# Attention and Hyena gate on one core: q loaded in 1 KB runs with strided PSUM writes, all row maxima in one TensorE transpose, and a new instruction order

## The chip, the cores and the metric

The kernel runs on one core of a Trainium2 chip. The metric is device time in microseconds; smaller is better. PE is TensorE, PEld its weight loads, DVE is VectorE, ACT is ScalarE, POOL is GpSimd and SP is SyncE, which here only issues DMAs. A time quoted below is a median of several runs; a profile is one execution, some 2 us shorter than the time of the same run, because it counts from the first to the last instruction. The profiled execution of the kernel before took 383.55 us, less than any of its timed runs, so its page shows that kernel at its best.

## The reference, cut to what matters

Eight batches of eight heads, 576 rows, head width 64, float32 in and out. First linear attention with a feature map that subtracts the row's largest absolute projection, then a Hyena layer on the result:

```python
def phi(x):
    proj = np.einsum('bhsd,df->bhsf', x, w_phi)
    proj = proj - np.max(np.abs(proj), axis=-1, keepdims=True)
    return np.concatenate([np.exp(proj), np.exp(-proj)], axis=-1)
q_p, k_p = phi(q), phi(k)
kv = np.einsum('bhsf,bhsd->bhfd', k_p, v)
z = np.sum(k_p, axis=2)
num = np.einsum('bhsf,bhfd->bhsd', q_p, kv)
den = np.einsum('bhsf,bhf->bhs', q_p, z)[..., None] + 1e-06
# x = num / den, heads joined to 512 columns; then for each batch
x1, x2, x3 = split(x @ w_proj, 3)
x2_conv = irfft(rfft(x2) * rfft(filter))       # along the 576 rows
out = (x1 * x2_conv * x3) @ w_out
```

The order of rows is free for k and v, because they are summed over rows. It isn't free for q: the result's rows enter a Fourier transform.

## The kernel before: the parts that matter

A "unit" is half a batch (four heads), so there are 16. The program fixes for each engine the sequence of its instructions. The kernel builds a list of about 2,500 named nodes and emits them by a literal table `ORDER`; a second table, `SLOTS`, says which of the eight PSUM banks each result uses. Both came from an offline planner.

k and v are loaded with four consecutive rows per partition, 1 KB runs in DRAM. q keeps plain row order (chunk `ci` holds rows 128 ci to 128 ci + 127), and so has 256-byte runs and four loads:

```python
def main(dst, src, g0, g1):                      # k and v
    nc.gpsimd.dma_start(
        out=dst[:, g0:g1].rearrange("p g h c d -> p (g h) (c d)"),
        in_=src[b, 4 * g0:4 * g1, 0:512, :].rearrange("h (p c) d -> p h (c d)", c=4))
def f_q(ci, g0, g1):                             # q, for ci in range(4)
    def f():
        nc.gpsimd.dma_start(
            out=c.qs[:, g0:g1, :, ci].rearrange("p g h d -> p (g h) d"),
            in_=q[b, 4 * g0:4 * g1, ci * P:(ci + 1) * P, :].rearrange("h p d -> p h d"))
```

The maximum of each row of q is found with rows on the partitions, but has to be subtracted with features on the partitions. It is split into two bf16 parts (`M2`), transposed by a DMA (by PE in the first two units), and subtracted by a matmul that accumulates onto the projection in PSUM. (It is subtracted twice over because the first exponential reads the bank before the subtraction: both exponentials of a row then carry the same factor, which cancels in `num / den` but for the 1e-06.)

```python
nc.sync.dma_start_transpose(out=c.mT[i2], in_=c.M2[i2].rearrange("p c h e -> p (c h e)"))
def f_pqa(hp, j):                                # the projection
    def f():
        pp = c.bank(f"{n}pq{hp}{j}", [P, 4, P], FP32)
        for e in range(2):
            nc.tensor.matmul(pp[:, e:4:2, :], lhsT=c.wpp[:, e * P:(e + 1) * P],
                             rhs=qT(hp + 2 * j), start=(e == 0), stop=True, ...)
def f_pqb(hp, j):                                # minus twice the maximum
    def f():
        nc.tensor.matmul(c.open[f"{n}pq{hp}{j}"].rearrange("f c p -> f (c p)"),
                         lhsT=c.sel[:, 2 * hp + j, :],
                         rhs=c.mT[i2][:, 0:4, :].rearrange("p c q -> p (c q)"),
                         start=False, stop=True, ...)
def f_q(hp, j, sg):                              # ScalarE: exp of the bank
    def f():
        nc.scalar.activation(E("q" + "pm"[sg], hp)[:, j],
                             c.open[f"{n}pq{hp}{j}"].rearrange("f c p -> f (c p)"),
                             AF.Exp, bias=0.0, scale=(1.0, -1.0)[sg])
```

Two more places matter. POOL weights v by the maxima of k, 96 multiplies that read SBUF (L765 and L805). DVE multiplies spectra with the filter, both operands in SBUF (L1031, and the sums of its products at L1037):

```python
nc.gpsimd.tensor_tensor(out=v12[:, sg, :, 0:HD]..., in0=c.vs[b % 2][...], in1=v12[..., 64:65]..., op=ALU.mult)
TT(out=p[:, sl, :], in0=c.CS[:, sl, :], in1=H[:, sl, :], op=ALU.mult)      # TT = nc.vector.tensor_tensor
```

Of the kernel before, what the change touches and what calls it, by code (L numbers as in the profile page):

```python
# [16 lines left out]
P = 128  # L17
# [31 lines left out]
class Node:  # L49
# [3 lines left out]
    def __init__(self, name, eng, ns, need, fn, take=(), use=(), lat=0, tab=0, at=0.0):  # L53
        self.name, self.eng, self.ns, self.need, self.fn = name, eng, ns, list(need), fn
        self.take, self.use, self.lat, self.tab, self.at = list(take), list(use), lat, tab, at

# [17 lines left out]
def const_nodes(c, w_phi, w_proj, filt, w_out):  # L74
# [21 lines left out]

    def f_sel():

        c.sel = tile_([P, 4, P], "sel")
        nc.vector.memset(c.sel, 0.0)  # L100
        for h in range(4):
            nc.vector.memset(c.sel[32 * h:32 * h + 2, h, :], -2.0)

    def f_m2():
        c.M2, c.mxq = [], []
        for i in range(2):
            t = tile_([P, 5, 4, 32], f"M2_{i}")
            nc.vector.memset(t, 0.0)
            c.M2.append(t)
            t = tile_([P, 5, 4], f"mxq_{i}", FP32)  # L110
            nc.vector.memset(t, 0.0)
            c.mxq.append(t)
# [29 lines left out]
    A("sel", "DVE", 950, [], f_sel)  # L142
    A("M2z", "DVE", 820, [], f_m2)
# [16 lines left out]
    def f_w(g, j):  # L160
        def f():
            if (g, j) == (0, 0):
                c.wproj = tile_([P, 4, 1536], "wproj")
            nc.gpsimd.dma_start(out=c.wproj[64 * j:64 * j + 64, 2 * g:2 * g + 2, :],
                                in_=wv[g, j])
        return f
# [12 lines left out]
    for g in range(2):  # L179
        for j in range(2):  # L180
            A(f"wi{g}{j}", "POOL", 680, ["wi00"] if g + j else [], f_w(g, j))
            A(f"w{g}{j}", "DMA", 2200, [f"wi{g}{j}"], None, lat=6000)
# [4 lines left out]
def trig_nodes(c):  # L187
# [118 lines left out]
    A("thalf", "DVE", 800, [f"t{i}{j}" for i in range(2) for j in range(2)], f_half)  # L306
# [11 lines left out]
def fold_nodes(c, name, need, need_g, get_x, get_eo, get_G, k0, at=None):  # L318
# [19 lines left out]
    def rem():  # L338
# [3 lines left out]
    c.add(n + "f1", "DVE", dve2(578), need, level1(0, ALU.add))  # L342
    c.add(n + "f2", "DVE", dve2(578), need, level1(1, ALU.subtract))
    c.add(n + "f3", "DVE", dve2(580), [n + "f1", n + "f2"] + need_g,
          level2(slice(0, 4, 3), ALU.add))
    c.add(n + "f4", "DVE", dve2(580), [n + "f1", n + "f2"] + need_g,
          level2(slice(1, 3), ALU.subtract))
    c.add(n + "fr", "DVE", 113, [n + "f3", n + "f4"], rem)
# [23 lines left out]
def spectrum_nodes(c):  # L372
# [93 lines left out]
    for i in range(2):  # L466
        A(f"f.swi{i}", "SP", 80, ["f.fix4"], f_sw(i))
        A(f"f.sw{i}", "XB", 100, [f"f.swi{i}"], None, lat=2500)
    A("f.cp0", "DVE", 345, ["f.S2", "f.S3"], f_cp(0))
    A("f.cp1", "DVE", 345, ["f.S0", "f.S1", "f.fix0"], f_cp(1))  # L470
# [15 lines left out]
def load_nodes(c, b, q, k, v):  # L486
# [18 lines left out]
    def f_q(ci, g0, g1):  # L505
        def f():
            nc.gpsimd.dma_start(  # L507
                out=c.qs[:, g0:g1, :, ci].rearrange("p g h d -> p (g h) d"),
                in_=q[b, 4 * g0:4 * g1, ci * P:(ci + 1) * P, :].rearrange("h p d -> p h d"))
        return f  # L510
# [16 lines left out]
    for (g0, g1) in ([(0, 1), (1, 2)] if b == 0 else [(0, 2)]):  # L527
# [12 lines left out]
        dma("k", 830, wk, f_k(g0, g1), 1400 * w)  # L540
        for hp in range(2):
            dma(f"kt{hp}", 600, wk, f_t(lambda: c.kt, k, hp, g0, g1), 200)
        for ci in range(4):
            dma(f"q{ci}", 750 if w == 1 else 865, wq, f_q(ci, g0, g1), 600 * w)
        for hp in range(2):
            dma(f"qt{hp}", 620, wq, f_t(lambda: c.qt, q, hp, g0, g1), 200)
        c.now = t0 + (2.0 if b == 0 else 8.0)
        dma("v", 830, wv, f_v(g0, g1), 1400 * w)
        for g in gs:
            for hp in range(2):  # L550
                dma(f"vt{hp}{g}", 590, wv + ["vtz"], f_vt(hp, g), 100)
        if b:
# [11 lines left out]
            A(n + "kx", "XB", 2500, [n + "kxi"], None, lat=2500)  # L564
            wx = [f"a{2 * b - 4 + i}.{x}{h}{j}" for i in range(2) for h in range(2)
                  for j in range(2) for x in ("pqa", "qn")] if b > 1 else []
            A(n + "qxi", "SP", 1300, [f"{s}q{i}" for i in range(4)] + wx,
              f_x(lambda: c.qT, lambda: c.qs))
            A(n + "qx", "XB", 2500, [n + "qxi"], None, lat=2500)
# [7 lines left out]
            A(n + "txi", "SP", 1600, [f"{s}{x}{h}" for x in ("kt", "qt") for h in range(2)] + wx,  # L577
              f_tx)
            A(n + "tx", "XB", 1000, [n + "txi"], None, lat=2500)
# [3 lines left out]
def attn_nodes(c, t, tune):  # L583
# [31 lines left out]
    if b == 0:  # L615
# [32 lines left out]
        A(n + "qtp", "PE", 8 * mm(P), [f"{l}q{i}" for i in range(4)] + ["ident"],  # L648
# [51 lines left out]
    def f_mx0():  # L700
        nc.vector.tensor_copy(c.M2[i2][:, :, :, 0], mxq())

    def f_mx1():
        nc.vector.tensor_tensor(out=c.M2[i2][:, :, :, 1], in0=mxq(),
                                in1=c.M2[i2][:, :, :, 0], op=ALU.subtract)

    def f_mt():
        nc.sync.dma_start_transpose(out=c.mT[i2],
                                    in_=c.M2[i2].rearrange("p c h e -> p (c h e)"))

    at(4.5)
    A(n + "mx0", "DVE", 80, [f"{n}qm{hp}{j}" for hp in range(2) for j in range(2)] + [n + "tm"]
      + unit("mt"), f_mx0)
    A(n + "mx1", "DVE", 100, [n + "mx0"], f_mx1)
    sels = ["tlb"] + [f"pqb{hp}{j}" for hp in range(2) for j in range(2)]
    if t in c.pe_mt:
        def f_mtp():
            tp = c.bank(n + "mtp", [P, 5, P], BF16)
            for ci in range(5):
                nc.tensor.transpose(tp[:, ci, :],  # L720
                                    c.M2[i2][:, ci].rearrange("p h e -> p (h e)"), c.ident)

        def f_mtc():
            nc.vector.tensor_copy(c.mT[i2], c.open[n + "mtp"])
        A(n + "mtp", "PE", 5 * mm(P), [n + "mx1", "ident"], f_mtp, take=[n + "mtp"])
        A(n + "mt", "DVE", dve2(640), [n + "mtp"] + unit(*sels), f_mtc, use=[n + "mtp"])
    else:
        A(n + "mti", "SP", 1300, [n + "mx1"] + unit(*sels), f_mt)
        A(n + "mt", "XB", 1600, [n + "mti"], None, lat=2400)
# [43 lines left out]
    for hp in range(2):  # L773
# [9 lines left out]
        for sg in range(2):  # L783
            A(f"{n}c{sg}{hp}", "ACT", 95, [f"{n}ra{hp}0", f"{n}ra{hp}1"]
              + back(hp, ["kv{}"]), f_c(hp, sg), tab=TAB_EXP)
            A(f"{n}v{sg}{hp}", "POOL", pool(512), [f"{n}c{sg}{hp}", vl] + back(hp, ["kv{}"]),
              f_v(hp, sg), lat=70)
# [28 lines left out]
    def f_tlb():  # L816
        for j in range(2):
            nc.tensor.matmul(c.open[n + "tq"][:, j, :], lhsT=c.sel[:, j, :],
                             rhs=c.mT[i2][:, 4, :], start=False, stop=True,
                             skip_group_check=True)  # L820
# [9 lines left out]
    for sg in range(2):  # L830
# [5 lines left out]
          + unit("kv0", "kv1"), f_vt(sg), lat=70)  # L836
# [7 lines left out]
    def f_pqa(hp, j):  # L844
        def f():
            pp = c.bank(f"{n}pq{hp}{j}", [P, 4, P], FP32)
# [6 lines left out]
    def f_pqb(hp, j):  # L853
        def f():
            nc.tensor.matmul(c.open[f"{n}pq{hp}{j}"].rearrange("f c p -> f (c p)"),
                             lhsT=c.sel[:, 2 * hp + j, :],
                             rhs=c.mT[i2][:, 0:4, :].rearrange("p c q -> p (c q)"),
                             start=False, stop=True, skip_group_check=True)
        return f

    def f_q(hp, j, sg):
        def f():
            nc.scalar.activation(E("q" + "pm"[sg], hp)[:, j],
                                 c.open[f"{n}pq{hp}{j}"].rearrange("f c p -> f (c p)"),
# [64 lines left out]
    for hp in range(2):  # L929
        at(12.0 + 4 * hp)  # L930
        A(f"{n}kv{hp}", "PE", 20 * mm(65), [f"{n}{x}{hp}{j}" for x in ("e0", "e1")
# [5 lines left out]
        for j in range(2):  # L937
            k = f"{n}ne{hp}{j}"
            A(k, "PE", 10 * mm(65), [f"{n}kvs{hp}", f"{n}q0{hp}{j}", f"{n}q1{hp}{j}",
# [37 lines left out]
    else:  # L977
# [11 lines left out]
        A(n + "xx", "XB", 2200, [n + "xxi"], None, lat=2400)  # L989
    A(n + "x0", "DVE", 80 if t in c.pe_xt else 170, [n + x for x in xx], f_x0)  # L990
# [6 lines left out]
def moe_nodes(c, b, out_b, tune):  # L997
# [62 lines left out]
    for i in range(2):  # L1060
        A(f"{n}p{i}4", "DVE", dve2(512), [n + "cs4"]
          + prev(*[f"{'ab'[i]}{m}" for m in range(4)]), f_p(i, slice(4, 5)))
        A(f"{n}p{i}0", "DVE", dve2(1024), [n + "cs0", n + "cs1"] + prev(f"y{i}"),
          f_p(i, slice(0, 2)))
        A(f"{n}p{i}2", "DVE", dve2(1024), [n + "cs2", n + "cs3"] + prev(f"y{i}"),
          f_p(i, slice(2, 4)))
        A(f"{n}y{i}", "DVE", dve2(1024), [f"{n}p{i}0", f"{n}p{i}2"]
          + prev(*[f"{'ab'[i]}{m}" for m in range(4)]), f_y(i))
# [71 lines left out]
    for m in range(4):  # L1140
        def old2(ev):
# [12 lines left out]
          + prev(*[f"fi{i}" for i in five], d=2), f_yt(m))  # L1154
# [35 lines left out]
PE_MT = (0, 1)  # L1190
SLOTS = (
    "0123456720436140177625763745703754167426342647536201364570127302731456136125473532514351"
    "0642571065063013407543750237564276512630754613750621357317420756210505301635023750375312"
    "0152407120435612074360254102346102541054073215637127251675162514365234614506150732410357"
    "2057142536721540673214671536725041741672376241072610421407531426730453156320514731247653"
    "0124604167231540732626253057126045724607236415072037132570650713560427601452761457350724"
    "3671045045365413061061064056235042573462517043214536751406732510465265401252475472315436"
    "0146210346245246325763415672014750132061423705612306453405340534057321467530217460")
ORDER = [
    74, 11, 6, 75, 7, 90, 94, 1, 88, 78, 86, 26, 0, 40, 27, 383, 64, 52, 66, 54, 30, 55, 53,  # L1200
    42, 32, 67, 50, 65, 16, 38, 28, 34, 4, 36, 33, 51, 2, 29, 43, 41, 31, 39, 35, 37, 5, 3,
    60, 58, 62, 18, 56, 12, 68, 22, 14, 20, 46, 44, 17, 76, 82, 96, 8, 77, 477, 481, 387, 482,
    384, 81, 385, 386, 403, 391, 63, 59, 57, 61, 84, 87, 97, 91, 95, 80, 83, 92, 93, 89, 79,
    13, 15, 388, 392, 478, 404, 389, 407, 395, 393, 390, 394, 396, 415, 497, 479, 419, 501,
    480, 498, 416, 420, 410, 409, 405, 427, 430, 428, 499, 417, 422, 500, 406, 503, 418, 449,
    397, 398, 408, 399, 98, 485, 437, 99, 109, 100, 400, 486, 101, 483, 110, 102, 413, 431,
# [261 lines left out]
```

## Time and profile before

| | before |
|---|---|
| time, median of 4 | 390.04 us (387.0 to 391.36) |
| profiled span (of a run of 383.55 us) | 381.4 us |
| PE, DVE, ACT, POOL busy | 83%, 85%, 71%, 49% |
| granted TensorE clock, mean | 0.955 |

From the page of the kernel before: the busy table, the row of the granted clock in 40 slices (tenths of full speed), and the chain of waits, followed back from the last instruction.

```profile
PE 318.3 (83%) x3071; PEld 198.3 (52%) x3071; DVE 324.2 (85%) x732; ACT 271.6 (71%) x667; POOL 188.5 (49%) x236
...
PEclk9998698898999999999999996998999999999999
...
DVE 41%; PE 37%; DMA 9%; ACT 6%; POOL 3%; issue 3%; DVEq 0%; ACTq 0%; POOLq 0%
```

No engine is full, and the chain changes hands between DVE and PE. The table of stretches, for the whole middle (start and end, length, busy time of each engine with its instruction count, clock, DMA share, GB/s):

```profile
210.00:340.00 130.00, 114.69 (x1130) 71.24 (x1128) 108.74 (x234) 99.32 (x245) 57.72 (x67) 0.96 0.69 97
```

Part of DVE's time is spent standing still. In the timeline around 203 us (start, length, instruction) a product that takes 0.68 us alone takes 1.54 us beside one of POOL's multiplies, and this multiply takes 1.50 us where the one before it took 1.05. Each holds the other up; below I call this the lock:

```profile
202.62 0.72 DVE L1031 TENSOR_TENSOR P_960<-CS,H_122 128x1024 bf16<-128x1024 bf16 x1 [0.24 <-ACT CS L1026]
...
202.76 1.50 POOL L765 TENSOR_TENSOR v_105<-vs_71,v_105 128x512 bf16<-128x512 bf16 x1
...
203.26 1.54 DVE L1031 TENSOR_TENSOR P_959<-CS,H_121 128x1024 bf16<-128x1024 bf16 x1
204.73 0.68 DVE L1031 TENSOR_TENSOR P_960<-CS,H_122 128x1024 bf16<-128x1024 bf16 x1
```

The groups of DVE instructions, kept apart by shape (count, busy us, mean ns of one, idle time before), show how much that is over the run:

```profile
L1031 DVE TENSOR_TENSOR P_959<-CS,H_121 128x1024 bf16<-128x1024 bf16 x16 | 20.4, 1287 | 0.3 <-ACT CS L1026 0.3
L1031 DVE TENSOR_TENSOR P_960<-CS,H_122 128x1024 bf16<-128x1024 bf16 x16 | 15.1, 948 | 8.3 <-ACT CS L1026 8.3
```

The mean over these 32 products is (1287 + 948) / 2 = 1118 ns against 680 alone. I call the difference "excess": for each shape of DVE instruction, the sum of its durations less its count times its fastest-tenth duration. Over all shapes the kernel before has 49 us of it. The view of DMA issues (size and microseconds to landing) has the q loads in fours, from POOL's queue:

```profile
qs<-in_q_dram POOLq DMA_DIRECT2D x28, 128.0 KB, 4.7
```

### The profile page before, as it was taken

To read this page: it belongs to the slowest core of one execution; us is meant where nothing else is said; L and a number is where in the kernel's file an instruction comes from. 1 tells how busy PE (TensorE), PEld (TensorE's weight loads), DVE (VectorE), ACT (ScalarE), POOL (GpSimd) and SP (SyncE) were. 2 spreads that over 40 slices of the span, in tenths; PEclk is the share of its full clock that TensorE was granted. 3 is DMA by queue.
4 is the path that set the end of the run, shared out by engine and by line. 5 is a ranking of instruction groups with operands and counts; after the bars stand their busy time and mean duration, and the time that the engine had idled before them with its cause. 6 is when DMAs were issued, how large, how long until landed. Compare 5 with 4: busy or idle time off the path is not lost.

```text
span 381.4 us, 8240 instructions
## 1 busy us (share of the span) xinstructions
PE 318.3 (83%) x3071; PEld 198.3 (52%) x3071; DVE 324.2 (85%) x732; ACT 271.6 (71%) x667; POOL 188.5 (49%) x236
## 2 busy tenths in 40 slices
PE   1367496988989699899989977959998899989994
PEld 0245473456735476467535643537645664566551
DVE  7998998899995899799989877697995998699391
ACT  1377576686978579798869873856989678975552
POOL 9958969187274921578073930794028201830000
PEclk9998698898999999999999996998999999999999
DMA  5999989958699996399954599698970038200023
GB/s 46 130 181 138 157 131 146 186 92 89 86 211 161 104 120 155 92 103 177 177 85 76 39 134 264 63 112 62 154 183 19 5 96 140 50 2 30 27 70 125
DMA packets 131640, 42.13 MB, mean 110 GB/s; under 512 B 108880, under 2 KB 126480, under 8 KB 131600
## 3 DMA queue, kind: packets, MB, share of 16 engines
q0 software_dynamic: 65264, 16.88, 48.1%
q1 hardware_dynamic: 66336, 24.72, 32.1%
q8 instruction: 24, 0.39, 0.4%
q14 instruction: 16, 0.13, 0.1%
HBM read 33.75 MB, written 9.44 MB: 113 GB/s over the span
## 4 chain that ended last, share of the span: by engine, by line
DVE 41%; PE 37%; DMA 9%; ACT 6%; POOL 3%; issue 3%; DVEq 0%; ACTq 0%; POOLq 0%
DVE P_959 L1031 5%; DVE P_960 L1031 5%; DVE Y L1037 3%; DVE ts L1096 2%; DMA filt<-in_moe_filter_fft_dram 2%; DVE mxq_269 L672 2%; DMA xT_113<-xn_112 2%; ACT CS L1026 2%; DMA out_dram<-o_118 2%; DVE mxq_273 L672 2%; DVE xn_112 L922 2%; DVE mxk_81 L742 2%; DVE mxk_82 L742 2%; DMA wproj<-in_moe_w_proj_dram 2%; DVE yT_1087 L1136 1%
## 5 line engine op out<-in xcount | busy, mean ns | idle before, releaser
L1072 PEld LDWEIGHTS <-wproj 128*128 128x128 bf16 x512 | 34.5, 100 | 32.4 <-issue 9.4
L765 POOL TENSOR_TENSOR v_103<-vs_71,v_103 128x512 bf16<-128x512 bf16 x12 | 12.9, 1075 | 44.0 <-ACT v_103 L756 43.9
L507 POOL DMA_DIRECT2D qs<-in_q_dram x36 | 32.5, 914 | 2.0 <-DMA wproj<-in_moe_w_proj_dram 2.0
L765 POOL TENSOR_TENSOR v_104<-vs_72,v_104 128x512 bf16<-128x512 bf16 x12 | 13.9, 1159 | 37.3 <-ACT v_104 L756 28.5
L1031 DVE TENSOR_TENSOR P_960<-CS,H_122 128x1024 bf16<-128x1024 bf16 (+1 forms) x24 | 20.4, 851 | 8.3 <-ACT CS L1026 8.3
L1031 DVE TENSOR_TENSOR P_959<-CS,H_121 128x1024 bf16<-128x1024 bf16 (+1 forms) x24 | 24.9, 1049 | 0.3 <-ACT CS L1026 0.3
L765 POOL TENSOR_TENSOR v_104<-vs_71,v_104 128x512 bf16<-128x512 bf16 x10 | 11.2, 1129 | 16.8 <-ACT v_104 L756 16.8
L765 POOL TENSOR_TENSOR v_105<-vs_72,v_105 128x512 bf16<-128x512 bf16 x10 | 11.0, 1104 | 16.1 <-issue 15.0
L1120 PEld LDWEIGHTS <-Y 128*128 128x128 bf16 x128 | 13.2, 104 | 9.8 <-issue 5.3
L848 PEld LDWEIGHTS <-wpp 128*128 128x128 bf16 x128 | 11.7, 99 | 10.2 <-issue 4.6
L765 POOL TENSOR_TENSOR v_103<-vs_72,v_103 128x512 bf16<-128x512 bf16 x10 | 10.9, 1092 | 10.5 <-ACT v_103 L756 10.5
L765 POOL TENSOR_TENSOR v_105<-vs_71,v_105 128x512 bf16<-128x512 bf16 x10 | 11.7, 1180 | 7.0 <-ACT v_105 L756 7.0
L515 POOL DMA_DIRECT2D kt<-in_k_dram x18 | 11.8, 660 | 2.7 <-PE pk_380 L736 2.7
L1160 PEld LDWEIGHTS <-yT_1087 128*128 128x128 bf16 x80 | 7.6, 97 | 9.5 <-DVE yT_1087 L1136 2.1
L515 POOL DMA_DIRECT2D qt<-in_q_dram x18 | 11.6, 649 | 1.0 <-DMA wproj<-in_moe_w_proj_dram 1.0
L1015 PEld LDWEIGHTS <-G_726 128*128 128x128 bf16 x64 | 6.0, 98 | 11.4 <-DVE G_726 L334 3.1
L621 PE MATMUL ktp<-ident,ks 128*128 128x128 bf16 x16 | 2.1, 311 | 11.5 <-DMA ks<-in_k_dram 11.5
L523 POOL DMA_DIRECT2D vt_137<-in_v_dram x16 | 10.1, 632 | 2.3 <-ACT Ekp_87 L749 2.3
L1160 PEld LDWEIGHTS <-yT_1086 128*128 128x128 bf16 x80 | 7.5, 97 | 6.1
L805 POOL TENSOR_TENSOR vt_106<-vt_137,emt_83 128x260 bf16<-128x260 bf16 x8 | 5.2, 659 | 11.0 <-ACT emt_83 L798 11.0
L523 POOL DMA_DIRECT2D vt_133<-in_v_dram x16 | 10.1, 629 | 0.6 <-DMA vs_71<-in_v_dram 0.6
L1015 PEld LDWEIGHTS <-G_723 128*128 128x128 bf16 x64 | 6.1, 97 | 8.0 <-issue 1.8
(2122 smaller groups left out, 1384.8 us busy)
## 6 DMA issues: line engine op xcount, KB each, us to landing
qs<-in_q_dram POOLq DMA_DIRECT2D x28, 128.0 KB, 4.7
ks<-in_k_dram POOLq DMA_DIRECT2D x7, 512.0 KB, 7.0
out_dram<-o_118 SPq DMA_DIRECT2D x11, 256.0 KB, 2.3
out_dram<-o_120 SPq DMA_DIRECT2D x11, 256.0 KB, 2.2
out_dram<-o_119 SPq DMA_DIRECT2D x10, 256.0 KB, 2.6
vs_72<-in_v_dram POOLq DMA_DIRECT2D x4, 512.0 KB, 7.6
wproj<-in_moe_w_proj_dram POOLq DMA_DIRECT2D x4, 384.0 KB, 7.7
vs_71<-in_v_dram POOLq DMA_DIRECT2D x3, 512.0 KB, 7.3
```

The lines of the kernel that those rows point to most:

```text
L507: nc.gpsimd.dma_start(out=c.qs[:, g0:g1, :, ci].rearrange("p g h d -> p (g h) d"), in_=q[b, 4 * g0:4 * g1, ci * P:(ci + 1) * P, :].rearran ...
L515: nc.gpsimd.dma_start(out=dst()[64 * hp:64 * hp + 64, g0:g1].rearrange("p g j d -> p (g j) d"), in_=sv[hp, 512:SEQ, 2 * g0:2 * g1, :])
L523: nc.gpsimd.dma_start(out=c.vt[b % 2][64 * hp:64 * hp + 64, g, hp, :, 0:HD], in_=sv[hp, 512:SEQ, 2 * g:2 * g + 2, :])
L672: nc.vector.tensor_reduce(out=mxq()[:, 0:4, 2 * hp + j], in_=c.open[f"{n}qn{hp}{j}"], axis=AX.X, op=ALU.max, apply_absolute_value=True)
L742: nc.vector.tensor_reduce(out=c.mxk[i2][:, 8 * hp + 4 * j:8 * hp + 4 * j + 4], in_=c.open[f"{n}pk{hp}{j}"], axis=AX.X, op=ALU.max, apply_a ...
L765: nc.gpsimd.tensor_tensor(out=v12[:, sg, :, 0:HD].rearrange("p (j c) d -> p j c d", j=2), in0=c.vs[b % 2][:, g, hp:hp + 3:2], in1=v12[:, s ...
L848: nc.tensor.matmul(pp[:, e:4:2, :], lhsT=c.wpp[:, e * P:(e + 1) * P], rhs=qT(hp + 2 * j), start=(e == 0), stop=True, skip_group_check=True)
L1015: nc.tensor.matmul(acc, lhsT=rem_block(c.G[b % 2], m, kt), rhs=c.wproj[:, kt, 512:1024], start=(kt == 0), stop=(kt == 3))
L1031: TT(out=p[:, sl, :], in0=c.CS[:, sl, :], in1=H[:, sl, :], op=ALU.mult)
L1072: nc.tensor.matmul(acc, lhsT=c.wproj[:, kt, base + m * P:base + (m + 1) * P], rhs=xT()[:, kt, s0:s1], start=(kt == 0), stop=(kt == 3))
L1120: nc.tensor.matmul(acc, lhsT=Y, rhs=c.IV[:, kt, 0:HALF], start=(i == 0), stop=(i == 2))
L1160: nc.tensor.matmul(acc, lhsT=c.yT[b % 2][:, kt, ci * P:(ci + 1) * P], rhs=c.wout[:, kt, :], start=(kt == 0), stop=(kt == 3))
```

## The change

Three things. **(1)** q is loaded like k and v, one load of 1 KB runs: partition p holds rows 4p to 4p + 3. To get the rows back into order, the projection and its correction are written to PSUM at a step of four floats (16 bytes), so that ScalarE reads the bank straight through. **(2)** The 20 columns of maxima lie side by side, in two parts, so one 128 x 128 transpose on PE and a 128-column copy on DVE replace the transposing DMA. `sel` grows to 20 selectors, and a correction becomes four matmuls of 128 columns. **(3)** `ORDER` and `SLOTS` are new, from a planner that now takes into account which DVE and POOL instructions hold each other up (`lock=1` marks them; it has no effect on the program but by the order).

```diff
-        for ci in range(4):
-            dma(f"q{ci}", 750 if w == 1 else 865, wq, f_q(ci, g0, g1), 600 * w)
+        dma("q", 830, wq, f_q(g0, g1), 2000 * w)          # f_q: main(c.qs, q, g0, g1)
...
+    def f_mtp():
+        nc.tensor.transpose(c.bank(n + "mtp", [P, P], BF16), c.M2[i2], c.ident)
+    def f_mtc():
+        nc.vector.tensor_copy(c.mT[i2], c.open[n + "mtp"])
-        A(n + "mti", "SP", 1300, [n + "mx1"] + unit(*sels), f_mt)
-        A(n + "mt", "XB", 1600, [n + "mti"], None, lat=2400)
...
-            pp = c.bank(f"{n}pq{hp}{j}", [P, 4, P], FP32)
+            pp = c.bank(f"{n}pq{hp}{j}", [P, 512], FP32).rearrange("f (p c) -> f c p", c=4)
...
-            nc.tensor.matmul(c.open[f"{n}pq{hp}{j}"].rearrange("f c p -> f (c p)"), ...
+            pp = c.open[f"{n}pq{hp}{j}"].rearrange("f (p c) -> f c p", c=4)
+            for ci in range(4):
+                nc.tensor.matmul(pp[:, ci, :], lhsT=c.sel[:, 4 * ci + 2 * hp + j, :],
+                                 rhs=c.mT[i2], start=False, stop=True, skip_group_check=True)
...
-SLOTS = ( ... )   ORDER = [ ... ]      # 2543 nodes
+SLOTS = ( ... )   ORDER = [ ... ]      # 2490 nodes, all re-ordered
```

## The prediction

> **What bounds the kernel now.** Two engines together, not the DMA. The busy table gives PE 83%, DVE 85%, ACT 71%, POOL 49% of 381.4 us; in the table of stretches, from 90 to 330 us, PE is busy 81 to 98%, DVE 75 to 92%. The chain of waits is DVE 41%, PE 37%, DMA 9%, POOL 3%. Matmul columns summed at the traced 216 ns per 512 make about 280 us of PE streaming; most of the slack lies before 66 us, where the chain runs over POOL issues, a wproj landing (5.9 us), the filter landing (9.3 us) and a transposing DMA (8.2 us).
>
> **The lock.** The 128x1024 products (L1031) take 0.68 us alone, at worst 2.79; their groups average 0.85 and 1.05 us. Taking each shape's fastest tenth as its own time, DVE's excess sums to about 49 us; instructions over 120 ns late hold 38 us of it where a POOL multiply overlaps, only 3.5 us beside POOL's DMA issues alone. The Trainium skill ("SBUF — State Buffer", "Who interferes with whom") says a DVE instruction with two SBUF inputs and a GpSimd one that reads SBUF exclude each other; this trace agrees: a product stretched to 1.54 us beside two POOL multiplies of 1.06 us. The products are 10% of the chain, so this excess is nearly all critical.
>
> **Costs and savings.**
> - q loads: 36 POOL issues of 0.91 us become 9, -24 us of POOL; six of them fall before 20 us, where POOL's issues are the chain: -3 to -5 us. DMA busy falls by an estimated 35 us per engine (128-byte packets of 35 ns against 512-byte ones of 67 ns), off the critical path later.
> - Maxima: 14 transposing DMAs (1.2 us issue, 2.6 to 3.2 us landing) go; 16 transposes of 0.1 us on PE and 16 copies of 0.15 us on DVE come; ten transposes and two 0.49 us copies go. The maxima instructions lose some of 6 us of excess: -1 to -3 us.
> - Correction matmuls: 64 of 512 columns become 256 of 128, same columns; the 55 ns cadence at L818 says weight loads hide: 0 to +3 us.
> - Strided PSUM writes: 65,000 columns, 27 us of PE at full rate. The skill ("PSUM — Partial Sum Buffer", cachelines row of its table) says non-contiguous patterns slow matmuls significantly; no run here shows it. At double time PE gains 27 us. I give that one chance in three, as the plan still costs them at full rate.
> - sel on ACT: 2.2 us by the plan, once, early.
> - New order: I expect half to two thirds of the lock excess to go, 20 to 27 us of DVE; with PE near full in the middle, 10 to 14 us reach the span.
>
> **Sum.** -4 head, -12 lock, -2 maxima, +3 for the risk of strides: 373 us, 8 times in 10 between 357 and 388. Faster by over 2%: 0.73; within 2%: 0.20; slower by over 2%: 0.07.
>
> **What would show it.** Right: q issues x9, landing near 7 us; POOL busy near 164 us; DVE busy 295 to 308 us; L1031 mean 0.75 us or less; first x projections before 63 us; PE cadence at the strided lines still 108 and 55 ns. Wrong: DVE above 318 us; strided cadence 200 ns or more with PE busy up by over 15 us; new PE waits on the copy of the transposed maxima.
>
> **What would make it wrong.** Slow strided writes; an order planned for durations the chip doesn't keep, so that locks only move; PE being the true limit (then a gain under 8 us); or the reorder filling the early hole better than I think (then under 360 us). TensorE's granted clock, 0.76 at 30 to 50 us, could move either way.

## The result, and the profile after

The changed kernel takes 369.65 us, median of 4 (367.18 to 370.88), against 390.04: the ratio is 0.948, with a 95% interval of 0.940 to 0.956. A ratio here is the mean time of one kernel's fast runs over the mean of the other's fast runs in the same rounds, so it isn't quite the ratio of the medians. (One core alone has no die to compare it with: "slow" here only means over 1.5% above the fastest run of the same kernel.)

The same three lines of the page of the changed kernel, and its stretch from 210 to 340 us:

```profile
PE 334.6 (91%) x3269; PEld 222.1 (60%) x3269; DVE 310.4 (84%) x742; ACT 279.4 (76%) x669; POOL 163.2 (44%) x209
...
PEclk9999996989999999999999999999999999999999
...
PE 68%; DVE 19%; ACT 6%; DMA 4%; issue 2%; POOL 1%; POOLq 0%; ACTq 0%
```

```profile
210.00:340.00 130.00, 130.00 (x1401) 90.35 (x1400) 111.89 (x276) 107.42 (x260) 51.81 (x62) 1.00 0.49 86
```

PE is now busy without a gap in that stretch, and the chain is PE for two thirds. But PE's busy time rose by 16 us (318.3 to 334.6), though the number of columns that it streams is almost the same. The timeline shows where. One unit's projection of two matmuls of 256 columns, then two corrections of four matmuls of 128 columns:

```profile
121.62 0.59 PE L839 MATMUL pq_1862<-qT_75,wpp 128*128 128x256 bf16 x2
122.01 0.64 PE L848 MATMUL pq_1783<-mT_79,sel 128*128 128x128 bf16 x4
122.45 0.64 PE L848 MATMUL pq_1810<-mT_79,sel 128*128 128x128 bf16 x4
```

Four matmuls of 128 columns take 122.45 - 122.01 = 0.44 us from start to start, 109 ns each. Contiguous ones of 128 columns stand 55 to 56 ns apart in the kernel before (L818), here two in 203.11 - 203.00 = 0.11 us:

```profile
203.00 0.28 PE L818 MATMUL tq<-mT_79,sel 128*128 128x128 bf16 x2
203.11 0.38 PE L848 MATMUL pq_3097<-qT_75,wpp 128*128 128x256 bf16 x2
203.32 0.38 PE L855 MATMUL pq_2879<-mT_79,sel 128*128 128x512 bf16 x1
```

The strided ones take twice the time. Over the whole run the median distance after a projection of 256 columns is 216 ns, after 109 before. (In the timeline the distance from start to start is what a matmul costs; the lengths overlap.)

On DVE, the products have lost part of their excess, but not all:

```profile
L1022 DVE TENSOR_TENSOR P_940<-CS,H_122 128x1024 bf16<-128x1024 bf16 x16 | 15.3, 964 | 3.3 <-ACT CS L1017 3.3
L1022 DVE TENSOR_TENSOR P_941<-CS,H_123 128x1024 bf16<-128x1024 bf16 x16 | 11.5, 717 | 9.3 <-ACT CS L1017 9.3
```

Their mean is (964 + 717) / 2 = 841 ns, after 1118. The sums of those products (L1028) got worse, 985 ns after 815 before. The excess of all DVE instructions is 31 us, after 49. The q loads are fewer:

```profile
qs<-in_q_dram POOLq DMA_DIRECT2D x7, 512.0 KB, 6.5
```

### The profile page after: what moved, and what is told of

It reads as the page before. It is cut to its first block, busy times and chain, and to the rows that moved or that the text cites. A ratio compares the mean times of both kernels' runs of the same rounds, so it can differ in the third digit from the quotient of the medians.

```text
span 369.1 us, 8592 instructions
## 1 busy us (share of the span) xinstructions
PE 334.6 (91%) x3269; PEld 222.1 (60%) x3269; DVE 310.4 (84%) x742; ACT 279.4 (76%) x669; POOL 163.2 (44%) x209
## 4 chain that ended last, share of the span: by engine, by line
PE 68%; DVE 19%; ACT 6%; DMA 4%; issue 2%; POOL 1%; POOLq 0%; ACTq 0%
DMA xT_113<-xn_111 2%; DVE ts L1087 2%; DVE P_940 L1022 2%; DMA xT_115<-xn_112 1%; DVE P_941 L1022 1%; DVE mxq_141 L673 1%; DVE Y L1028 1%; DVE r L277 1%; DVE eof L333 1%; DVE eo_116 L333 1%; ACT CS L1017 1%; DVE mxk_82 L734 1%; PE tk L681 1%; DVE mxk_81 L734 1%; ACT IV L283 1%
## 5 line engine op out<-in xcount | busy, mean ns | idle before, releaser
L848 PEld LDWEIGHTS <-sel 128*128 128x128 bf16 x256 | 26.8, 126 | 5.0 <-issue 0.6
L1022 DVE TENSOR_TENSOR P_941<-CS,H_123 128x1024 bf16<-128x1024 bf16 (+1 forms) x24 | 14.5, 616 | 9.3 <-ACT CS L1017 9.3
L1022 DVE TENSOR_TENSOR P_940<-CS,H_122 128x1024 bf16<-128x1024 bf16 (+1 forms) x24 | 18.6, 782 | 3.3 <-ACT CS L1017 3.3
L1151 PEld LDWEIGHTS <-yT_1018 128*128 128x128 bf16 x80 | 7.7, 98 | 8.5 <-DVE yT_1018 L1127 1.6
L1151 PEld LDWEIGHTS <-yT_1017 128*128 128x128 bf16 x80 | 7.6, 99 | 6.7
L728 PEld LDWEIGHTS <-kT_73 128*128 128x128 bf16 x64 | 6.7, 113 | 7.1 <-DVE kT_73 L630 2.6
L1006 PEld LDWEIGHTS <-G_624 128*128 128x128 bf16 x64 | 6.1, 99 | 7.5 <-DVE G_624 L340 1.3
L667 PEld LDWEIGHTS <-qT_75 128*128 128x128 bf16 x64 | 6.6, 113 | 6.0 <-DVE qT_75 L630 1.5
```

Source lines behind the costliest of these rows:

```text
L848: nc.tensor.matmul(pp[:, ci, :], lhsT=c.sel[:, 4 * ci + 2 * hp + j, :], rhs=c.mT[i2], start=False, stop=True, skip_group_check=True)
L1151: nc.tensor.matmul(acc, lhsT=c.yT[b % 2][:, kt, ci * P:(ci + 1) * P], rhs=c.wout[:, kt, :], start=(kt == 0), stop=(kt == 3))
```

## The experiments

Twelve kernels ran, in three groups of four, each group on one chip with the kernel before beside it. Each group had a median of the kernel before between 389.9 and 391.1 us, so medians of different groups are compared here; in each group one to four of the seven runs of before counted as slow. One of the four runs of e6, e7 and e9 and two of e8 counted as slow too; without them the medians are 358.12, 367.02 and 354.63 us, and the mean of e8 is 385.7.

### e1: no strides, ScalarE reads at a step

```diff
 # on the changed kernel
-            pp = c.bank(f"{n}pq{hp}{j}", [P, 512], FP32).rearrange("f (p c) -> f c p", c=4)
+            pp = c.bank(f"{n}pq{hp}{j}", [P, 4, P], FP32)
-            pp = c.open[f"{n}pq{hp}{j}"].rearrange("f (p c) -> f c p", c=4)
+            pp = c.open[f"{n}pq{hp}{j}"]
-            nc.scalar.activation(E("q" + "pm"[sg], hp)[:, j], c.open[f"{n}pq{hp}{j}"], ...
+            nc.scalar.activation(E("q" + "pm"[sg], hp)[:, j].rearrange("f (p c) -> f p c", c=4),
+                                 c.open[f"{n}pq{hp}{j}"].rearrange("f c p -> f p c"), ...
```

> The changed kernel with the strided PSUM writes undone: the q-side projections and corrections are written in contiguous runs of 128 columns, and ScalarE restores the row order by reading PSUM at a 512-byte step. Same order, same node counts. Theory S (the strides double the time of 65,536 columns, about 27 us of PE, and PE is the limit in the second half): cadences return to 108 and 55 ns, PE busy falls by 20 us or more, time 352 to 363 us. Rival H (the strided time hides behind DVE): 367 to 371 us. If ScalarE reads a strided PSUM slowly, its 128 instructions of 0.60 us grow instead and the time stays or rises.

Measured: 354.69 us (353.77 to 355.33), correct, ratio to before 0.917 (0.903 to 0.931). The four runs are all below the four of the changed kernel, so it beats both; 369.65 - 354.69 = 15 us is what the strides cost there. In its timeline ten matmuls like those above:

```profile
119.23 0.38 PE L839 MATMUL pq<-qT,wpp 128*128 128x256 bf16 x2
119.45 0.61 PE L848 MATMUL pq<-mT,sel 128*128 128x128 bf16 x8
```

Two projections take 119.45 - 119.23 = 0.22 us from start to the next start, and eight corrections end after 0.61 us, where four took 0.64. Page of e1:

```profile
PE 311.6 (88%) x3269; PEld 203.4 (58%) x3269; DVE 308.4 (87%) x742; ACT 274.0 (78%) x669; POOL 162.9 (46%) x209
...
PE 44%; DVE 35%; ACT 11%; DMA 5%; issue 3%; POOL 1%; ACTq 0%; POOLq 0%; DVEq 0%
```

PE's busy time falls by 23 us (334.6 to 311.6) and PE's share of the chain from 68% to 44%. And the step costs ScalarE next to nothing. In its groups, the first line reads PSUM at a 512-byte step, the second straight through:

```profile
L854 ACT ACTIVATE Eqm<-pq 128x512 bf16<-128x512 f32 x64 | 39.0, 626 | 3.3 <-PE pq L848 3.1
L741 ACT ACTIVATE Ekp<-pk 128x512 bf16<-128x512 f32 x64 | 38.9, 621 | 0.9 <-PE pk L728 0.5 <-DVE mxk L734 0.3
```

The same instruction can be compared too: the 128 exponentials of q take 616 ns on average in the kernel before, straight through, and 616 ns in e12 below, at the step. Theory S holds.

### e2 and e12: the q change alone, in the old order

e2 is the kernel before with one q load and strided PSUM writes; its order is the old one with the four q issues merged at the place of the first. e12 is e2 without strides, by ScalarE's stepped read.

```diff
 # on the kernel before: e2
-            dma(f"q{ci}", ...)                       # four of them
+        dma("q", 830, wq, f_q(g0, g1), 2000 * w)
+  pp = ... .rearrange("f (p c) -> f c p", c=4)       # in f_pqa and f_pqb, as in the change
 # e12: pp = c.bank(..., [P, 4, P], FP32), and ScalarE reads "f c p -> f p c", as in e1
```

> The kernel before, in its old order, with the q change alone: one q load of 1 KB runs in place of four of 256 bytes, and strided PSUM writes; maxima still by transposing DMAs. Theory O (the new order carries the gain, the strides cost): 388 to 402 us, slower or equal, though POOL is 24 us less busy. Rival W (fewer POOL issues carry the gain): 376 to 384 us.

> e2 (the q change alone in the old order, 387.8 us) without the strided PSUM writes. Theory Q (fewer POOL issues and larger runs do help, and the strides ate that): 370 to 380 us. Rival: 384 us or more, the q loads were off the chain.

Measured: e2 387.77 us (384.79 to 388.37), ratio 1.002 (0.988 to 1.016); e12 385.14 us (381.13 to 385.45), ratio 0.986 (0.977 to 0.996). POOL's busy time fell from 188.5 to 164.5 us in e2 and that moved the time by nothing clear; without strides the q change is worth 1.4%, some 5 us. Theory O's range for e2 was just missed (388 was its lower end), rival W is out. For e12 the rival's time holds (384 or more) and theory Q is out, but "off the chain" is too strong for a ratio whose interval lies below 1. In this order the strides cost 387.77 - 385.14 = 2.6 us, not clear of the spread, though PE is busy 336.3 us in e2 and 316.4 in e12. Some of this hides in PE's slack, and some in the clock: the granted clock is 0.976 to 0.982 in e2's runs and 0.948 to 0.957 in e12's. As an estimate from the two profiles, 383.6 x 0.046 less 385.7 x 0.024 is 8 us less of PE time lost to half clock with the strides.

### e3, e4, e5 and e11: the work without the order

e3 is the maxima change alone in the old order. e4 is the changed kernel's whole work in the old order. The old order has no place for the PE transpose and its copy, so I had to choose one: in e3 and e4, both where the DMA was issued. e5 is e4 with the copy where the old plan had that DMA land, and the transpose as shortly before it as a free PSUM bank allowed. e11 is e5 without strides.

```diff
 # on the changed kernel's tables (names for numbers)
-ORDER = the new order
+ORDER = the old order, with q0i..q3i -> qi, and
+   e3, e4:  mti -> mtp, mt              # the transpose and the copy at once
+   e5, e11: mti -> (nothing), mt -> mtp, mt   # both late, mtp earlier where a bank is free
-SLOTS = the new banks
+SLOTS = the old banks, and for each mtp a bank that is free until its copy
 # e3 also: q in four loads, [P, 4, P] banks    # e11 also: the edit of e1
```

> The kernel before, in its old order, with the maxima change alone: one TensorE transpose and a 128-column copy in place of the transposing DMA, corrections as four matmuls of 128 columns, contiguous; q still in four loads. Theory O: 385 to 391 us, the same as before, since those DMAs were not on the chain. Rival M (the transposing DMAs' latency was hidden in the chain through TensorE's queue): 376 to 383 us.

> The changed kernel's work (q change, maxima change, strides) in the old order of instructions and the old PSUM banks. Theory O (order carries the gain): 388 to 402 us, as the strides cost PE 27 us and the locks stay (excess of DVE durations above 40 us). Rival W (the work removed carries it): 368 to 376 us, close to the changed kernel.

> As e4_old_order, but each copy of the transposed maxima stands where the old plan had the transposing DMA land, and its TensorE transpose just before it, as e4's VectorE waited 20 us for these transposes, a fault of my placing. Theory O (the order carries the gain): still 390 us or more. Rival P (e4 was slow only because of that placing): 376 us or less, near the changed kernel's 370.

> e5 (all the change's work in the old order, 404.8 us) without the strided PSUM writes, ScalarE reading at a step as in e1. If the strides cost the same there as in the new order (15 us): 387 to 393 us, so that the work without strides is worth nothing in the old order, and the order is worth 33 to 38 us. If the old order has holes that hide PE time: 396 us or more.

Measured: e3 404.24 us, ratio 1.046 (1.033 to 1.059); e4 403.62 us, 1.043 (1.027 to 1.058); e5 404.82 us, 1.036 (1.029 to 1.043); e11 392.05 us, 1.008 (0.998 to 1.018). Both expectations for e3 missed, and e4 is 2 us above theory O's 388 to 402. From the list of who waited for whom in e4 and in e5:

```profile
DVE mT L713 <- PE mtp L710: 19.6, 5, 6.8
```

```profile
DVE mxk L734 <- PE pk L728: 15.3, 6, 5.2
...
DVE mT L713 <- PE mtp L710: 6.4, 4, 1.9
```

In e4 DVE stood 19.6 us before the copies of the transposed maxima; e5 cut that to 6.4 us, and the time didn't fall, because DVE waited for other work of PE instead. So my placing isn't the whole reason, yet it can't be excluded as a part of e3's 14 us: the old order was planned for a transpose that PE doesn't do. That the maxima change is worth something by itself is not shown by any run; in the old order it is worth nothing or less.

Theory O holds in the main: with the strides, the same work takes 404.8 us in the old order and 369.65 in the new, 35 us; without, 392.05 and 354.69, 37 us. Both figures count against the old order whatever my placing costs. From e12, which needed no placing, to e1 it is 385.14 - 354.69 = 30 us, for the maxima change and the order together; if the maxima change by itself is worth nothing or less, the order is worth between 30 and 37 us. Without strides and without the new order, the whole change comes to 392.05 against 391.07 for before in the same rounds, nothing. The strides cost 404.82 - 392.05 = 13 us here.

### e6, e7, e9 and e10: without POOL's SBUF reads

Is it the lock that the order avoids? Take away what makes DVE wait: POOL's multiplies become memsets of the same tiles, which write but don't read. Their outputs are wrong, which doesn't matter for the times.

```diff
 # e6 on before, e7 on the changed kernel; the 260-column multiply alike
-            nc.gpsimd.tensor_tensor(out=v12[:, sg, :, 0:HD]..., in0=..., in1=..., op=ALU.mult)
+            nc.gpsimd.memset(c.v12[pair(hp) % 3][:, sg], 1.0)
 # e9 on before, e10 on e1: each memset twice
+            for _ in range(2):
+                nc.gpsimd.memset(c.v12[pair(hp) % 3][:, sg], 1.0)
```

> Wrong result on purpose. The kernel before, with its 96 POOL multiplies replaced by memsets of the same tiles, which read no SBUF; all else as it was. Theory L (the lock costs the old order): the 128x1024 products go to a mean of 0.69 us, DVE's excess falls from 49 to below 15 us, and the time falls by 15 to 30 us, to 360 to 374 us. Rival N (DVE's stretches are filled from slack): 382 us or more.

> Wrong result on purpose. The changed kernel with the same replacement. Theory L (the new order already avoids the locks that matter): the time falls by under 8 us, to 362 us or more, although DVE's excess falls from 31 to below 12 us. If it falls as far as e6 does, the new order avoided no lock that matters, and its gain lies in other waits.

> Wrong result on purpose. As e6, but each memset is done twice, since one takes 0.53 us where the multiply takes 1.06: POOL is now as busy as before, and only its SBUF reads are gone. Theory L (what e6 gained is the lock): 355 to 366 us, like e6's 359. Rival D (e6 gained by shorter POOL work): 375 us or more.

> Wrong result on purpose. e1 (new order, no strided PSUM writes) with the same doubled memsets: does the lock still cost time in the new order once PE is relieved? Theory L2 (the lock was hidden behind PE in the changed kernel, and comes back without the strides): 338 to 348 us against e1's 354.7. Rival L3 (the new order keeps the lock off the chain in either case): 350 us or more.

Measured: e6 359.13 us, ratio 0.917 (0.907 to 0.927); e7 367.65 us, 0.940 (0.932 to 0.947); e9 355.86 us, 0.908 (0.896 to 0.920); e10 343.81 us, 0.883 (0.876 to 0.890). One memset took 545 ns on average, where a multiply's median was 1059; e9 shows that this shortness wasn't the reason, since POOL is busy 179 us in it and it is no slower than e6. A memset also no longer waits for the loads of v, but in POOL's waits before no multiply waits for such a load. The busy line and the chain of e9:

```profile
PE 307.5 (87%) x3027; PEld 196.5 (55%) x3071; DVE 287.6 (81%) x732; ACT 270.1 (76%) x667; POOL 179.3 (50%) x332
...
PE 62%; DMA 19%; DVE 8%; POOL 5%; ACT 4%; issue 2%; DVEq 0%; ACTq 0%; POOLq 0%
```

DVE's share of the chain is 8%, after 41% in the kernel before. The products in e9, then in e11, which has the lock and the old order:

```profile
L1025 DVE TENSOR_TENSOR P<-CS,H 128x1024 bf16<-128x1024 bf16 x32 | 20.5, 683 | 9.2 <-ACT CS L1020 9.2
```

```profile
L1022 DVE TENSOR_TENSOR P<-CS,H 128x1024 bf16<-128x1024 bf16 x32 | 33.4, 1089 | 7.6 <-ACT CS L1017 7.6
```

683 ns is the time of a product alone. Theory L holds in e6, e7 and e9, with e6 1 us below its range, and L2 in e10. DVE's excess is 14 us in e6 and 10 in e7. As a table, medians in microseconds:

| | with the lock | POOL reads nothing | the lock costs |
|---|---|---|---|
| old order, the work of before | 391.07 | 355.86 (e9) | 35 |
| new order, strides | 369.65 | 367.65 (e7) | 2 |
| new order, no strides (e1) | 354.69 | 343.81 (e10) | 11 |

(e7 has single memsets, and its runs overlap those of the changed kernel, so its 2 us are not clear of zero.) In the second row the lock seems harmless, but there PE's strided writes set the pace. Take them away and 11 us of lock are on the chain again, as theory L2 expected. By this table the new order removes 35 - 11 = 24 us of lock cost; the new work in the old order was not run without POOL's reads. The excess that goes with POOL's reads is 49 us in the kernel before less 9 in e9, 40 us, of which 35 reached the time; in the new order it is 31 in e1 less 10 in e10, 21 us, of which 11 reached it. (e11, the new work in the old order, has 43 us of excess.) Part of the 35 us may have gone by way of the clock, 0.931 to 0.949 in the runs of before and 0.961 to 0.969 in e9's; how much is not shown. So the order avoids some of the locks and lays others where DVE isn't what the rest waits for. Without any lock the new kernel's work and order are still 355.86 - 343.81 = 12 us ahead.

### e8: one of the holes in the old order

At 225 us, the old order has a stretch where the output store waits behind transposing DMAs in SP's queue, ACT waits for its buffer and PE for ACT. e8 gives the output a fourth buffer.

```diff
 # on the kernel before
+        c.o.append(c.moe.tile([P, DM], FP32, name="o3"))
-            nc.scalar.copy(c.o[(5 * b + ci) % 3][0:rows, :], c.open[f"{n}fi{ci}"][0:rows, :])
+            nc.scalar.copy(c.o[(5 * b + ci) % 4][0:rows, :], c.open[f"{n}fi{ci}"][0:rows, :])
```

> The kernel before with four buffers for output rows in place of three. At 225 us an output store took 7.3 us behind transposing DMAs, ScalarE waited 5.3 us for its buffer, PE ran dry and came back at half clock. Theory B (that hole is one of the things which the new order removed): the hole shrinks, 378 to 385 us. Rival: the wait moves to the next buffer or to PE, 386 to 391 us.

Measured: 390.09 us (383.58 to 393.13), against 389.94 for before; but two of the four runs counted as slow, and the ratio by the other two is 0.987 (0.976 to 0.998). The runs spread more than the effect. ScalarE's list of waits still has the store:

```profile
ACT o L1168 <- DMA out_dram<-o: 4.3, 1, 4.3
```

It was 5.3 us before, so a fourth buffer takes away 1 us of it. The rival's 386 to 391 us fits the median, the two fast runs (383.58 and 387.88) lie on both sides of the line between the theories, so e8 decides nothing and what the hole costs stays open.

## Why the prediction was right, and which terms were not

The time, 369.65 us, lies within 357 to 388 and 3 us from the 373 predicted, and the change is faster by over 2%. But two terms of the sum were far off, and in opposite directions: taken with e11 and e1, the order gave -37 where -12 was predicted, and the strides +15 where +3 was. That the sum came within 3 us is luck. The strides even met a sign that the prediction had set down for being wrong: a strided cadence of 200 ns or more (216) with PE busy up by over 15 us (16).

- **The order and the lock: predicted -12 us; measured -35 us** (404.8 in e5 to 369.65), or -37 us without strides; at least -30 if the cost of my placing is left out (e12 to e1). The mechanism was right: the lock was nearly all on the chain (35 us by e9, where I had read 38 us of late instructions beside POOL's multiplies), and about half of its excess went (40 to 21 us), where I had expected half to two thirds. The step that failed is "with PE near full in the middle, 10 to 14 us reach the span": I had discounted the gain by a busy PE. e6 and e9 show that PE in the kernel before was not a limit that holds such a gain back; without the lock that kernel loses 31 and 35 us at once. The change also brings gains other than the lock, 12 us by e9 and e10, of which I had counted 4 us at the head and 2 for the maxima; these 12 us are of the new work and the new order together, and e12 gives 5 us to the q loads.
- **The strides: predicted +3 us, as one chance in three of a doubling; measured +15 us.** The doubling is measured: 109 ns for 128 columns where contiguous ones take 55. I had the size of it right, 27 us of PE at full rate to be doubled, and PE's busy time differs by 23 us between the changed kernel and e1. The argument that failed was "the plan still costs them at full rate": that a planner assumes a cost is no evidence that it was measured. The Trainium skill said it plainly ("PSUM — Partial Sum Buffer", cachelines row of its table: any non-contiguous pattern slows matmuls significantly).
- **The head: predicted -4 us; about -7 us by the timelines.** The first projection of the second stage starts at 57.9 us after 64.6 before. In e12, the q loads in the old order, it starts at 61.4, so about half of the 7 us comes with the q loads; and the whole of e12 is some 5 us below before, the size of the predicted term.
- **The maxima: predicted -2 us; no gain shown.** Alone in the old order they cost 14 us (e3), with my placing as a possible part of it. The new order finds place for them.
- **Smaller readings.** Right: nine q issues, landing in 6.5 us; POOL busy 163.2 us; first projections before 63 us. Wrong: the cadence at the strided lines; DVE busy 310.4 us, just above the 295 to 308; the products' groups, now 616 and 782 ns by the page's grouping that I had used, one of them above 750.
- **The granted clock.** It rose from 0.955 to 0.986 in the profiles. As an estimate, 381.4 x 0.045 less 369.1 x 0.014 is 12 us less of PE time lost to half clock. In the kernel before there are seven half-clock records (3.4 or 6.8 us long) apart from the one at the very end. Five of them begin within 2 us after a gap of PE of 1.7 to 4.4 us, and two begin inside gaps of 3.1 and 1.9 us; three gaps of 1.7 to 2.2 us (near 113, 194 and 295 us) have no such record after them. The skill's page "TensorE: Matmul & The Clock Gate", Part 1, says that the clock falls to half after an idle window of about 3.4 us; this trace agrees only in part, as just one of these gaps, that of 4.4 us, is as long. I read the higher clock as a consequence of filled gaps that is part of the order's gain; e2 against e12 shows that strides, too, go with a higher clock. No run changes the clock alone, so how much of the 35 us it is stays open.

## What to carry to other kernels

When two engines hold each other up as here, the time lost is a property of the order: measure it by replacing one side by an instruction that doesn't take the lock (here a memset), and compare it with the sum of the late durations before you pay for a re-plan. Restore a row order where the stride is free: at a 16-byte step TensorE wrote PSUM at half rate, while ScalarE read PSUM at a 512-byte step at no cost, and moving the stride from one to the other took another 15 us off (354.69 us). A wait that costs 2 us under one limit can cost 11 once that limit is lifted, so test it again after each change of the limit.

## What the Trainium skill lacked or had wrong

- "PSUM — Partial Sum Buffer", cachelines row of its table, has no number for non-contiguous writes: here matmuls with float32 output at a 16-byte step took 109 ns instead of 55 for 128 columns, a factor of 2, and 15 us of 370 in all.
- No page that I read says that a stepped PSUM read by ScalarE can be free: at a 512-byte step it took 626 ns where a contiguous one of the same shape took 621.
- "SBUF — State Buffer", "Who interferes with whom", had it right that DVE with two SBUF inputs is held up by a GpSimd instruction that reads SBUF and not by one that only writes: a product took 1118 ns on average in the kernel with the multiplies, 683 in that with memsets. What it doesn't give is how much of the delay reaches the time: 35 us of about 40 us of delay in one order, 11 of 21 in another.
